# An attention forward and backward kernel on one core: its hand-written order of work replaced, from the first batch to the last

## The chip, the core and the metric

The kernel runs on one core of a Trainium2 chip. A core has a matrix engine (TensorE, PE in the profile, with its weight loads shown as PEld), a vector engine (VectorE, DVE), a scalar engine (ScalarE, ACT), a general engine (GpSimd, POOL) and a queue-only engine (SyncE, SP). 16 DMA engines move data between the chip's memory (DRAM) and the core's working memory (SBUF). Matmul results land in PSUM, here 8 banks of 2 KB in each of 128 partitions. The metric is device time in microseconds (us) for one launch. Three runs of the kernel before took 680.65, 680.86 and 682.24 us; the median is 680.86 us.

## The reference

Grouped-query attention with 32 batches, 32 query heads on 4 key heads, 4 queries and 2048 keys, head size 128, all in bf16; then its gradients.

```python
def _fwd_reference(q, k, v):              # q [32,32,4,128], k and v [32,4,2048,128]
    ...
    scores = jnp.einsum("bhqd,bhkd->bhqk", q, k) * scale
    p = _softmax(scores, axis=-1)
    return jnp.einsum("bhqk,bhkd->bhqd", p, v)

def reference(q, k, v, grad_out):
    ...
    _out, _vjp = jax.vjp(_f, q, k, v)
    return (out, dq, dk, dv)
```

In one batch K, V, dK and dV are 2 MB each, while q, grad_out, out and dq are 32 KB each, so a batch moves about 8.52 MB.

## The kernel before, in words

One batch is one unit of work. Its 32 x 4 queries fill the 128 partitions, 32 for each key head, and its 2048 keys are cut into two halves, called a (tile index 0) and b (tile index 1), of 1024 each. The kernel cuts the work of a batch into named items, each a Python function that issues a handful of instructions:

- LK and LV load K and V, four DMAs of 512 KB each on SP's queue (lines 226, 232). K has 3 buffers and V has 2 (lines 121, 122). The load of batch b+3's K waits for the last reader of batch b's K, which is dQ; V of batch b+2 waits for O of batch b. LV of batch 0 also issues, behind V, the q and grad_out rows of batches 1 to 3 (line 234); those of batch 0 come earlier on ScalarE's queue. Later groups of four batches are loaded by GpSimd inside LK (GROUP, lines 222 and 223), and a fence there makes GpSimd wait for them (line 221).
- QDT transposes q and grad_out of a batch (lines 245, 247).
- KT0 to KT7 and VT0 to VT7 each transpose an eighth of K or V: eight 128x128 transposes on TensorE into one bank (line 255) and one copy out of it (line 257). An even index needs key heads 0 and 1, an odd one heads 2 and 3.
- S makes the scores of a half (line 272) and their maximum (line 285). EX is the exponential on ScalarE, with the sum of a row (line 296). NRM inverts the sum (lines 311, 313), and GpSimd scales grad_out and q by it (lines 305, 316).
- ET and dST transpose the exponentials and the score gradients (lines 322, 324). O and dQ are the small products gathered over all keys, 64 matmuls each (line 338); O is followed by the sum called delta (line 365). dP forms a half's score gradient, ds (line 433).
- dV0 to dV7 and dK0 to dK7 each make an eighth of dV or dK: four matmuls into two banks (line 391) and a cast to bf16 in an SBUF tile (line 395). Indices 0 to 3 read half a, 4 to 7 read half b. When the eighth one is done, GpSimd issues the 2 MB store (lines 421, 188); for the last batch two stores of 1 MB go out. The dV and dK tiles share 4 buffers (line 129), so the first cast of a dK waits for the store of the dK two batches earlier.

Every engine works its own queue in the order in which the items are issued. Three strings give that order. HEAD lists the first three iterations with batch numbers. STEADY is one iteration, run for iterations 3 to 28; a "-" stands for the batch before, "+" for the batch after, "+2" for two after. TAIL lists the last three iterations, -1 being batch 31. The engine that empties a bank is in the name: a bare KT or VT copies on VectorE and one with "a" on ScalarE; a bare dV or dK casts on ScalarE and one with "d" on VectorE (lines 445 to 448). The class Banks hands out PSUM banks in issue order, the one longest free first. So an order also settles which earlier cast or copy each matmul group waits for.

Of the kernel before, what the change touches and what calls it, by code (L numbers as in the profile page):

```python
# [14 lines left out]


HEAD = """
LK@0 LV@0 KT4@0 KT6@0 KT2@0 KT0@0 QDT@0 KT3@0 KT1@0 KT5a@0 KT7@0 LK@1 LV@1 Sa@0 Sb@0 VT2a@0 VT4@0 VT0a@0 EXb@0 VT6@0 EXa@0 VT5@0 ETb@0 VT3@0 ETa@0
NRM@0 VT7a@0 VT1a@0 QDT@1 KT4@1 KT6@1 KT2a@1 KT0@1 KT3@1 dV7@0 O@0 dV5@0 dPb@0 dV1@0 KT5@1 KT1@1 dV3@0 dV6@0 dPa@0 KT7@1 dV2@0 LK@2 LV@2
VT2@1 dV4@0 Sa@1 dV0@0 Sb@1 dK7@0 VT5@1 VT3@1 EXb@1 dSTa@0 VT4@1 EXa@1 VT0@1 QDT@2 dSTb@0 KT4@2 dK1@0 dK6@0 KT6@2 KT2@2 KT0@2 NRM@1 dK0@0 dQ@0  # L20
dK3@0 dK5@0 dK2@0 ETb@1 ETa@1 VT7@1 KT3@2 VT6@1 VT1@1 dV7@1 dK4@0 O@1 dV5@1 dPb@1 dV1@1 KT5@2 KT1@2 dV3@1 dV6@1 dPa@1 KT7@2 dV2@1 LK@3 LV@3
VT2@2 dV4@1 Sa@2 dV0@1 Sb@2 dK7@1 VT5@2 VT3@2 EXb@2 dSTa@1 VT4@2 EXa@2 VT0@2 QDT@3 dSTb@1 KT4@3 dK1@1 dK6@1 KT6@3 KT2@3 KT0@3 NRM@2 dK0@1 dQ@1
dK3@1 dK5@1 dK2@1 ETb@2 ETa@2 VT7@2 KT3@3 VT6@2 VT1@2 dV7@2 dK4@1 O@2 dV5@2 dPb@2 dV1@2 KT5@3 KT1@3 dV3@2 dV6@2 dPa@2 KT7@3 dV2@2 LK@4 LV@4
VT2@3 dV4@2 Sa@3 dV0@2 Sb@3 dK7@2 VT5@3 VT3@3 EXb@3
"""
HEAD_ITERATIONS = 3
WARM_MATMULS = 23

STEADY = """
dSTa- VT4 EXa VT0 QDT+ dSTb- KT4+ dK1- dK6- KT6+ KT2+ KT0+ NRM dK0- dQ- dK3- dK5- dK2- ETb ETa VT7 KT3+ VT6 VT1  # L30
dV7 dK4- O dV5 dPb dV1 KT5+ KT1+ dV3 dV6 dPa KT7+ dV2 LK+2 LV+2 VT2+ dV4 Sa+ dV0 Sb+ dK7 VT5+ VT3+ EXb+
"""

TAIL = """
VT7@-3 VT6@-3 EXa@-3 dK5@-4 dSTa@-4 VT4@-3 NRM@-3 dSTb@-4 dK3@-4 KT0@-2 dK6@-4 KT6@-2 VT1@-3 dK4@-4 KT4@-2 dK1@-4 ETb@-3 KT1@-2 dK0@-4 ETa@-3 dQ@-4 QDT@-2 KT5@-2 dV5@-3
VT0@-3 dV1@-3 KT3@-2 O@-3 KT7@-2 dPa@-3 dV6@-3 dV7@-3 VT0@-2 KT2@-2 dV2@-3 dPb@-3 dK2@-4 VT4@-2 LK@-1 dSTa@-3 dV4@-3 dV0@-3 Sa@-2 dK1@-3 Sb@-2 dV3@-3 EXb@-2 VT3@-2
VT6@-2 VT5@-2 dSTb@-3 EXa@-2 dK3@-3 VT1@-2 ETb@-2 dK5@-3 NRM@-2 KT2@-1 dK7@-3 dQ@-3 LV@-1 VT2@-2 ETa@-2 dK0@-3 KT1@-1 dK4@-3 KT0@-1 KT6@-1 QDT@-1 dK2@-3 VT7@-2 O@-2
dV5@-2 dV3@-2 KT5@-1 dPa@-2 dV6@-2 KT4@-1 dK6@-3 KT3@-1 dV1@-2 dPb@-2 dV7@-2 KT7@-1 Sa@-1 dV2@-2 dV0@-2 Sb@-1 dV4@-2 dK1d@-2 dSTb@-2 EXb@-1 VT6@-1 EXa@-1 NRM@-1 dK7@-2  # L40
VT5@-1 dK4@-2 ETb@-1 VT1@-1 dK0@-2 VT7@-1 dK5@-2 dK3@-2 ETa@-1 dK6d@-2 dK2@-2 dV7@-1 VT0@-1 dV2d@-1 VT3@-1 dV5@-1 dSTa@-2 VT4@-1 O@-1 dV6@-1 dV4@-1 dV1d@-1 VT2@-1 dPb@-1
dV0@-1 dPa@-1 dV3@-1 dK4@-1 dQ@-2 dK3d@-1 dK2@-1 dK0d@-1 dK1@-1 dK5d@-1 dK7@-1 dK6@-1 dSTa@-1 dSTb@-1 dQ@-1
"""
TAIL_ITERATIONS = 3

# [457 lines left out]
```

## Time and profile before

| what | number |
|---|---|
| median of three runs | 680.86 us |
| the profiled execution | 680.64 us |
| its span, first to last instruction | 678.9 us |
| PE busy | 623.5 us, 92% |
| DVE busy | 589.8 us, 87% |
| ACT busy | 569.2 us, 84% |
| POOL busy | 273.0 us, 40% |
| moved by DMA | 274.45 MB, mean 404 GB/s |
| granted TensorE clock | 0.999 of full speed |

The profile is one execution of the kernel, and its page gives totals over the whole span. Stage by stage the numbers differ, so the trace is also read in windows, as a timeline of single instructions, and as a list of who waited for whom. In a timeline row the first number is the start and the second the time taken, x4 means four such instructions merged, and a bracket gives the idle time before them and what ended it ("issue" is idle time that nothing in the trace explains). Iteration 3 begins at about 69.5 us and the tail at about 605.3 us.

### The profile page before, as it was taken

The page shows a single profiled execution, that of the slowest core. Times are in us where ns is not written, and L with a number is a line of the kernel's source. Part 1 is how long each engine was busy: PE and PEld are TensorE (multiplying, and loading weights), DVE is VectorE, ACT ScalarE, POOL GpSimd, SP SyncE. Part 2 cuts the span into 40 slices and gives each one's busy share as a digit, 9 for nine tenths or more (in the row PEclk, how much of TensorE's full clock was granted, in tenths as well). Part 3 has the DMA queues.
Part 4 walks back from the last instruction along what each step waited for, and adds up shares of the span by engine and source line. Part 5 has one row for each costly group of instructions (what it writes and reads, how often), then busy time and mean ns, then how long its engine had stood idle before and what let it go on. Part 6 is the DMA issues. An engine that isn't in the chain of part 4 may idle for free.

```text
span 678.9 us, 28075 instructions
## 1 busy us (share of the span) xinstructions
PE 623.5 (92%) x12375; PEld 452.8 (67%) x12375; DVE 589.8 (87%) x997; ACT 569.2 (84%) x673; POOL 273.0 (40%) x457
## 2 busy tenths in 40 slices
PE   8999999999999989999999999999989899988984
PEld 6667776666776667776667776667666576655652
DVE  5889999988899888999989898988889888887895
ACT  3899889888888888989888888888888888886885
POOL 1353442544425444352545424364333643333310
PEclk9999999999999999999999999999999999999999
DMA  9999999999999999999999999999999999999888
GB/s 343 408 392 413 416 411 412 417 411 417 413 417 414 413 416 412 416 415 413 418 415 416 414 414 415 416 416 414 412 416 408 404 414 413 415 403 401 340 340 300
DMA packets 76970, 274.45 MB, mean 404 GB/s; under 512 B 8975, under 2 KB 9133, under 8 KB 76848
## 3 DMA queue, kind: packets, MB, share of 16 engines
q1 hardware_dynamic: 41920, 145.05, 53.3%
q0 software_dynamic: 34640, 127.55, 46.6%
q8 instruction: 96, 1.57, 0.8%
q14 instruction: 26, 0.21, 0.1%
q10 hardware_dynamic: 288, 0.07, 0.0%
HBM read 136.31 MB, written 136.31 MB: 402 GB/s over the span
## 4 chain that ended last, share of the span: by engine, by line
PE 70%; DMA 12%; ACT 6%; DVE 5%; issue 4%; POOL 1%; SPq 0%; ACTq 0%; DVEq 0%; POOLq 0%
PE banks L255 29%; PE banks L391 17%; PE banks L338 9%; DMA out_dram<-dk 8%; PE banks L322 8%; PE banks L272 7%; ACT dv L395 5%; DMA v_sb<-in_v_dram 2%; DVE ds L433 2%; DMA k_sb<-in_k_dram 1%; ACT dk L395 1%; DVE kt L257 1%; PE banks L245 1%; DVE dk L395 1%; DVE vt L257 1%
## 5 line engine op out<-in xcount | busy, mean ns | idle before, releaser
L395 ACT CAST dv<-banks 128x1024 bf16<-128x1024 f32 x254 | 244.2, 1026 | 56.6 <-PE banks L391 52.9
L395 ACT CAST dk<-banks 128x1024 bf16<-128x1024 f32 x251 | 246.1, 1022 | 22.1 <-PE banks L391 14.8
L257 DVE COPY kt<-banks 128x1024 bf16<-128x1024 bf16 x254 | 163.2, 680 | 12.1 <-PE banks L255 11.6
L257 DVE COPY vt<-banks 128x1024 bf16<-128x1024 bf16 x252 | 163.9, 681 | 1.4 <-PE banks L255 1.3
L305 POOL TENSOR_SCALAR dop<-do_sb,rinv 32x128 bf16<-32x128 bf16 x124 | 74.1, 598 | 200.4 <-PE banks L391 150.2
L255 PE MATMUL banks<-ident,v_sb 128*128 128x128 bf16 x2048 | 142.9, 219 | 12.7 <-ACT dv L395 10.2
L255 PE MATMUL banks<-ident,k_sb 128*128 128x128 bf16 x2048 | 143.6, 219 | 8.6 <-issue 5.9
L255 PEld LDWEIGHTS <-k_sb 128*128 128x128 bf16 x2048 | 119.3, 98 | 36.7 <-issue 34.8
L255 PEld LDWEIGHTS <-v_sb 128*128 128x128 bf16 x2048 | 121.3, 98 | 28.6 <-issue 25.9
L433 DVE SCALAR_TENSOR_TENSOR ds<-banks,delta,e 128x1024 bf16<-128x1024 f32 x64 | 82.0, 1283 | 25.9 <-PE banks L272 24.8
L391 PE MATMUL banks<-dop,e 64*128 64x256 bf16 x1024 | 96.2, 273 | 8.8 <-issue 3.2
L188 POOL DMA_DIRECT2D out_dram<-dv x56 | 39.2, 703 | 145.0 <-ACT dv L395 124.3
L391 PE MATMUL banks<-qp,ds 64*128 64x256 bf16 x1024 | 87.7, 271 | 2.4 <-DVE dk L395 1.2
L305 POOL TENSOR_SCALAR qp<-q_sb,srinv 32x128 bf16<-32x128 bf16 x128 | 77.7, 607 | 10.6
L296 ACT ACTIVATE e<-banks,negb 128x1024 bf16<-128x1024 f32 x64 | 70.8, 1112 | 9.8 <-DVE negb L288 9.7
L285 DVE TENSOR_REDUCE m<-banks 128x1 f32<-128x1024 f32 x64 | 75.1, 1215 | 0.7 <-PE banks L272 0.6
L391 PEld LDWEIGHTS <-e 64*128 64x128 bf16 x1024 | 34.1, 94 | 54.2 <-issue 37.5
L391 PEld LDWEIGHTS <-ds 64*128 64x128 bf16 x1024 | 41.9, 94 | 30.4 <-ACT dv L395 13.0
L324 DVE COPY et<-banks 128x1024 bf16<-128x1024 bf16 x64 | 41.8, 686 | 23.4 <-PE banks L322 22.9
L272 PE MATMUL banks<-vt,qdt 128*32 128x512 bf16 x512 | 41.3, 384 | 6.5 <-issue 4.8
L324 DVE COPY dst<-banks 128x1024 bf16<-128x1024 bf16 x64 | 43.4, 680 | 1.5 <-PE banks L322 1.5
L272 PEld LDWEIGHTS <-qdt 128*32 128x32 bf16 x1024 | 19.0, 94 | 35.2 <-issue 34.0
(45 smaller groups left out, 502.4 us busy)
## 6 DMA issues: line engine op xcount, KB each, us to landing
k_sb<-in_k_dram SPq DMA_DIRECT2D x128, 512.0 KB, 11.7
v_sb<-in_v_dram SPq DMA_DIRECT2D x128, 512.0 KB, 17.1
out_dram<-dk POOLq DMA_DIRECT2D x29, 2048.0 KB, 22.5
out_dram<-dv POOLq DMA_DIRECT2D x17, 2048.0 KB, 24.3
out_dram<-dv POOLq DMA_DIRECT2D x13, 1024.0 KB, 22.1
out_dram<-dv POOLq DMA_DIRECT2D x13, 960.0 KB, 25.5
out_dram<-dk SPq DMA_DIRECT2D x2, 2048.0 KB, 8.1
out_dram<-dv SPq DMA_DIRECT2D x1, 2048.0 KB, 9.0
```

The costliest lines, as they stand in the source:

```text
L255: nc.tensor.transpose(out=ps[:, 4 * hh + j, :], in_=S[which][:, 2 * (i % 2) + hh, 4 * (i // 2) + j, :], identity=ident[:])
L257: copy(out=S[f"{which}t{i}"][:], in_=ps)
L272: nc.tensor.matmul(ps[G * h:G * h + G, a, :], lhsT=S["qdt"][:, col, G * h:G * h + G], rhs=xt[:, 4 * (h % 2):4 * (h % 2) + 4, :].rearrange( ...
L285: nc.vector.reduce_max(out=S["m"][:, i:i + 1], in_=S[f"s{i}"][1], axis=AX.X)
L296: nc.scalar.activation(out=S[f"e{i}"][:], in_=ps, func=ACT.Exp, bias=S["negb"][:], scale=scale, accum_out=S["l"][:, i:i + 1],)
L305: engine.tensor_scalar(out=t[r, h % 2, :], in0=src[r, :], scalar1=by[r, :], scalar2=None, op0=ALU.mult)
L322: nc.tensor.transpose(out=ps[:, u, :], in_=S[f"{src}{i}"][:, P * u:P * u + P], identity=ident[:])
L324: nc.vector.tensor_copy(out=S[f"{name}{i}"][:], in_=ps)
L338: nc.tensor.matmul(ps[G * h:G * h + G, :], lhsT=S[f"{xt}{c // 8}"][:, c % 8, G * h:G * h + G], rhs=S[kv][:, h, c, :], start=(c == 0), stop ...
L391: nc.tensor.matmul(ps[:, a, :, c, :], lhsT=S[f"{x}{i // 4}"][r, u:u + P], rhs=S[y][r, :, :], start=True, stop=True, tile_position=(2 * G * ...
L395: copy(out=S[name][:, :, 2 * i:2 * i + 2, :].rearrange("p h c d -> p h (c d)"), in_=banks.ap(t).rearrange("p a (j w) -> p (a j) w", j=2),)
L433: nc.vector.scalar_tensor_tensor(out=S[f"ds{i}"][:], in0=ps, scalar=S["delta"][:], in1=S[f"e{i}"][:], op0=ALU.subtract, op1=ALU.mult,)
```

## The change

Only the three strings change; the functions and the amount of computation stay. In HEAD, STEADY and TAIL the same items stand in another order, and some change the engine that empties their banks.

```diff
 HEAD = """
-LK@0 LV@0 KT4@0 KT6@0 KT2@0 KT0@0 QDT@0 KT3@0 KT1@0 KT5a@0 KT7@0 LK@1 LV@1 Sa@0 Sb@0 VT2a@0 VT4@0 VT0a@0 EXb@0 VT6@0 EXa@0 VT5@0 ETb@0 VT3@0 ETa@0
-NRM@0 VT7a@0 VT1a@0 QDT@1 KT4@1 KT6@1 KT2a@1 KT0@1 KT3@1 dV7@0 O@0 dV5@0 dPb@0 dV1@0 KT5@1 KT1@1 dV3@0 dV6@0 dPa@0 KT7@1 dV2@0 LK@2 LV@2
-VT2@1 dV4@0 Sa@1 dV0@0 Sb@1 dK7@0 VT5@1 VT3@1 EXb@1 dSTa@0 VT4@1 EXa@1 VT0@1 QDT@2 dSTb@0 KT4@2 dK1@0 dK6@0 KT6@2 KT2@2 KT0@2 NRM@1 dK0@0 dQ@0
...
+LK@0 KT2@0 LV@0 KT6@0 QDT@0 KT0@0 KT4a@0 KT7@0 KT5a@0 LK@1 KT1@0 LK@2 KT3@0 QDT@1 Sb@0 VT2a@0 Sa@0 VT0a@0 VT6@0 VT1@0 EXa@0 VT7@0 EXb@0 VT3a@0 VT4@0
+LV@1 VT5a@0 ETa@0 NRM@0 KT2a@1 ETb@0 KT4@1 KT0a@1 KT6@1 O@0 KT5a@1 dPa@0 dV4@0 dPb@0 KT3a@1 dV3@0 LV@2 dSTa@0 KT7@1 dV6@0 dV0d@0 dK2@0 dV7@0 KT1@1 dV1d@0
+dV5@0 dSTb@0 Sa@1 dV2@0 Sb@1 dQ@0 VT3a@1 QDT@2 VT2@1 KT0@2 EXa@1 EXb@1 KT3@2 KT1@2 LK@3 NRM@1 VT6a@1 dK5@0 KT5@2 ETa@1 VT5@1 KT7a@2 ETb@1 VT1@1 VT4a@1
...
 STEADY = """
-dSTa- VT4 EXa VT0 QDT+ dSTb- KT4+ dK1- dK6- KT6+ KT2+ KT0+ NRM dK0- dQ- dK3- dK5- dK2- ETb ETa VT7 KT3+ VT6 VT1
-dV7 dK4- O dV5 dPb dV1 KT5+ KT1+ dV3 dV6 dPa KT7+ dV2 LK+2 LV+2 VT2+ dV4 Sa+ dV0 Sb+ dK7 VT5+ VT3+ EXb+
+dSTa- dSTb- VT7 VT0 EXa KT4a+ dQ- dK4- NRM dK6d- dK1- ETb VT6a KT0+ QDT+ dK3- dK5d- KT6+ dK2- VT1 dK0- ETa dV4 KT5+ dV6d dV1 VT4 LK+2
+dV3 O dV5 dPb dV7 dV0 LV+2 KT7+ KT3+ dV2 dPa KT1a+ KT2+ dK7 Sb+ VT2a+ Sa+ VT3a+ VT5+ EXb+
 """
...
 TAIL = """
...
-dV0@-1 dPa@-1 dV3@-1 dK4@-1 dQ@-2 dK3d@-1 dK2@-1 dK0d@-1 dK1@-1 dK5d@-1 dK7@-1 dK6@-1 dSTa@-1 dSTb@-1 dQ@-1
...
+dV6@-1 dV5@-1 dK0d@-2 VT0@-1 dV7@-1 VT7@-1 dK5@-2 dK6@-2 ETb@-1 dK1d@-2 VT1a@-1 VT2@-1 O@-1 dV1@-1 dV2@-1 dPa@-1 VT5@-1 VT4@-1 dV3@-1 dV0@-1 dK2@-1 dSTb@-2 dSTa@-2 dPb@-1 dK3@-1
+dK0@-1 dK1d@-1 dK4@-1 dK5@-1 dK6@-1 dK7d@-1 dQ@-2 dSTa@-1 dSTb@-1 dQ@-1
 """
```

Counted over the strings, an iteration of STEADY has 48 items before and after. ScalarE gets 5 copies of K and V (before 0) and VectorE 3 casts of dK and dV (before 0). HEAD has 153 items both times, with 21 such copies on ScalarE (before 6) and 9 such casts on VectorE (before 0). TAIL has 135 items, with 10 (before 0) and 12 (before 7). In HEAD batch 2's K is loaded ahead of batch 1's V, and QDT of batch 1 stands ahead of the scores of batch 0.

More of the change, by code (lines that the diff above doesn't have):

```diff
@@ L17 @@
 HEAD = """
-LK@0 LV@0 KT4@0 KT6@0 KT2@0 KT0@0 QDT@0 KT3@0 KT1@0 KT5a@0 KT7@0 LK@1 LV@1 Sa@0 Sb@0 VT2a@0 VT4@0 VT0a@0 EXb@0 VT6@0 EXa@0 VT5@0 ETb@0 VT3@0 ETa@0
-NRM@0 VT7a@0 VT1a@0 QDT@1 KT4@1 KT6@1 KT2a@1 KT0@1 KT3@1 dV7@0 O@0 dV5@0 dPb@0 dV1@0 KT5@1 KT1@1 dV3@0 dV6@0 dPa@0 KT7@1 dV2@0 LK@2 LV@2
-VT2@1 dV4@0 Sa@1 dV0@0 Sb@1 dK7@0 VT5@1 VT3@1 EXb@1 dSTa@0 VT4@1 EXa@1 VT0@1 QDT@2 dSTb@0 KT4@2 dK1@0 dK6@0 KT6@2 KT2@2 KT0@2 NRM@1 dK0@0 dQ@0
[L21 to L24, printed above, removed]
+LK@0 KT2@0 LV@0 KT6@0 QDT@0 KT0@0 KT4a@0 KT7@0 KT5a@0 LK@1 KT1@0 LK@2 KT3@0 QDT@1 Sb@0 VT2a@0 Sa@0 VT0a@0 VT6@0 VT1@0 EXa@0 VT7@0 EXb@0 VT3a@0 VT4@0
+LV@1 VT5a@0 ETa@0 NRM@0 KT2a@1 ETb@0 KT4@1 KT0a@1 KT6@1 O@0 KT5a@1 dPa@0 dV4@0 dPb@0 KT3a@1 dV3@0 LV@2 dSTa@0 KT7@1 dV6@0 dV0d@0 dK2@0 dV7@0 KT1@1 dV1d@0
+dV5@0 dSTb@0 Sa@1 dV2@0 Sb@1 dQ@0 VT3a@1 QDT@2 VT2@1 KT0@2 EXa@1 EXb@1 KT3@2 KT1@2 LK@3 NRM@1 VT6a@1 dK5@0 KT5@2 ETa@1 VT5@1 KT7a@2 ETb@1 VT1@1 VT4a@1
+VT0@1 dK3d@0 dV2@1 VT7@1 dV6@1 O@1 dV3@1 dPb@1 dV4@1 dV1@1 KT2@2 KT6@2 dV5@1 KT4@2 dV7@1 dPa@1 VT0a@2 Sb@2 dV0@1 Sa@2 dK0@0 KT7a@3 dSTa@1 dSTb@1 VT6@2
+EXa@2 VT5@2 EXb@2 NRM@2 VT1@2 dK6@0 dK1@0 dQ@1 dK4d@1 dK7@0 KT5@3 ETb@2 QDT@3 VT7a@2 dK2d@1 dK4@0 ETa@2 dK0@1 VT4@2 LV@3 dK3@1 KT3@3 KT6@3 dV7@2 dK7d@1
+dV3@2 O@2 dV4@2 dV0d@2 dV5@2 KT1@3 VT2a@2 dPb@2 dK1@1 VT3@2 LK@4 dK6d@1 KT0a@3 KT4@3 dV2@2 KT2a@3 dK5d@1 dV1@2 dPa@2 dV6@2 Sb@3 Sa@3 dK7@2 VT2a@3 VT3@3
+LV@4 VT5@3 EXb@3
 """
@@ L29 @@
 STEADY = """
-dSTa- VT4 EXa VT0 QDT+ dSTb- KT4+ dK1- dK6- KT6+ KT2+ KT0+ NRM dK0- dQ- dK3- dK5- dK2- ETb ETa VT7 KT3+ VT6 VT1
-dV7 dK4- O dV5 dPb dV1 KT5+ KT1+ dV3 dV6 dPa KT7+ dV2 LK+2 LV+2 VT2+ dV4 Sa+ dV0 Sb+ dK7 VT5+ VT3+ EXb+
+dSTa- dSTb- VT7 VT0 EXa KT4a+ dQ- dK4- NRM dK6d- dK1- ETb VT6a KT0+ QDT+ dK3- dK5d- KT6+ dK2- VT1 dK0- ETa dV4 KT5+ dV6d dV1 VT4 LK+2
+dV3 O dV5 dPb dV7 dV0 LV+2 KT7+ KT3+ dV2 dPa KT1a+ KT2+ dK7 Sb+ VT2a+ Sa+ VT3a+ VT5+ EXb+
 """
 TAIL = """
[L37 to L41, printed above, removed]
-dV0@-1 dPa@-1 dV3@-1 dK4@-1 dQ@-2 dK3d@-1 dK2@-1 dK0d@-1 dK1@-1 dK5d@-1 dK7@-1 dK6@-1 dSTa@-1 dSTb@-1 dQ@-1
+KT6@-2 dSTb@-4 dSTa@-4 VT7@-3 VT1@-3 EXa@-3 VT4a@-3 KT0@-2 NRM@-3 dK5@-4 dK6@-4 dQ@-4 VT0@-3 KT3@-2 dK0@-4 KT1@-2 dK2@-4 ETb@-3 QDT@-2 KT4@-2 dK4@-4 LK@-1 dV0@-3 ETa@-3 VT6@-3
+KT2@-2 dV6d@-3 dV5@-3 dV7@-3 O@-3 KT5a@-2 dPb@-3 dV1@-3 dPa@-3 dV4@-3 KT7@-2 QDT@-1 dV2@-3 LV@-1 dK3d@-4 dK1@-4 VT6a@-2 VT4@-2 Sb@-2 dV3@-3 dK2@-3 Sa@-2 KT0a@-1 KT4@-1 dSTa@-3
+KT6@-1 VT1@-2 EXb@-2 EXa@-2 VT3@-2 VT2@-2 dK5@-3 NRM@-2 ETb@-2 KT5a@-1 dK3@-3 KT1@-1 ETa@-2 KT2a@-1 VT5@-2 dK0d@-3 dK6@-3 VT7@-2 VT0a@-2 O@-2 dK7@-3 dV7d@-2 KT3a@-1 dPa@-2 dV5@-2
+dV3@-2 dSTb@-3 KT7@-1 dV1@-2 dK4d@-3 dV2@-2 dPb@-2 dK1@-3 dV4@-2 Sb@-1 dV0@-2 Sa@-1 dV6@-2 dK2d@-2 EXb@-1 EXa@-1 dK3d@-2 dQ@-3 dK7@-2 NRM@-1 VT6a@-1 dK4d@-2 ETa@-1 dV4@-1 VT3@-1
+dV6@-1 dV5@-1 dK0d@-2 VT0@-1 dV7@-1 VT7@-1 dK5@-2 dK6@-2 ETb@-1 dK1d@-2 VT1a@-1 VT2@-1 O@-1 dV1@-1 dV2@-1 dPa@-1 VT5@-1 VT4@-1 dV3@-1 dV0@-1 dK2@-1 dSTb@-2 dSTa@-2 dPb@-1 dK3@-1
+dK0@-1 dK1d@-1 dK4@-1 dK5@-1 dK6@-1 dK7d@-1 dQ@-2 dSTa@-1 dSTb@-1 dQ@-1
 """
```

## The prediction

> **What bounds the kernel now.** I first cut the span into stages (columns: start:end, length, then busy us and instruction count of PE, PEld, DVE, ACT, POOL, granted clock, DMA share, GB/s).
>
> ```profile
> 69.47:457.24 387.77, 365.68 (x7334) 267.22 (x7334) 346.65 (x590) 337.14 (x400) 171.25 (x280) 1.00 1.03 415
> 457.24:605.30 148.06, 134.53 (x2702) 98.40 (x2702) 127.20 (x218) 124.60 (x148) 60.89 (x100) 1.00 1.02 411
> 605.30:640.00 34.70, 32.20 (x660) 23.18 (x659) 29.40 (x51) 27.03 (x33) 13.74 (x24) 1.00 1.00 400
> 640.00:675.00 35.00, 27.32 (x524) 17.33 (x516) 29.23 (x44) 27.51 (x32) 3.14 (x6) 1.00 0.84 325
> ```
>
> In the steady stage the DMA engines are full: 415 GB/s, so a batch of 8.52 MB needs 20.5 us. The 26 iterations take (605.3-69.5)/26 = 20.6 us. TensorE is hardly slacker: 365.7 of 387.8 us. Only in the last 35 us do transfers wait for work, at 325 GB/s.
>
> Next the engines' own pace. By the timeline, iteration 274.41 to 294.25 took 19.84 us with one unexplained TensorE pause of 0.28 us ("issue"); such a pause comes once or twice an iteration, 0.3 to 1.0 us. Without it the order runs at 19.56 us. ScalarE waited for a store only four times:
>
> ```profile
> 490.22 1.01 ACT L395 CAST dv<-banks 128x1024 bf16<-128x1024 f32 x1 [1.93 <-DMA out_dram<-dv]
> 500.63 1.01 ACT L395 CAST dk<-banks 128x1024 bf16<-128x1024 f32 x1 [1.53 <-DMA out_dram<-dk]
> 541.99 1.01 ACT L395 CAST dk<-banks 128x1024 bf16<-128x1024 f32 x1 [0.22 <-DMA out_dram<-dk]
> 574.45 1.01 ACT L395 CAST dv<-banks 128x1024 bf16<-128x1024 f32 x1 [1.71 <-DMA out_dram<-dv]
> ```
>
> So engines and transfers run neck and neck. An order is worth what it changes in the head, in the pace, and in the tail.
>
> **The head: QDT of batch 1 ahead of the first scores.** The timeline of the first 20 us, and the page's DMA issues (last number: median us from issue to landing):
>
> ```profile
> 6.29 0.38 SPq L202 DMA_DIRECT2D q_sb<-in_q_dram  x1
> 6.72 0.49 SPq L202 DMA_DIRECT2D do_sb<-in_grad_out_dram  x1
> 8.72 1.74 PE L255 MATMUL banks<-ident,k_sb 128*128 128x128 bf16 x28 [0.51 <-DMA k_sb<-in_k_dram]
> 10.39 1.33 PE L272 MATMUL banks<-kt,qdt 128*32 128x512 bf16 x16
> 14.13 1.13 ACT L296 ACTIVATE e<-banks,negb 128x1024 bf16<-128x1024 f32 x1
> 17.85 0.22 PE L245 MATMUL banks<-ident,q_sb 128*128 128x128 bf16 x1
> ```
>
> ```profile
> q_sb<-in_q_dram SPq DMA_DIRECT2D x1, 96.0 KB, 9.0
> do_sb<-in_grad_out_dram SPq DMA_DIRECT2D x1, 96.0 KB, 8.9
> ```
>
> The rows of batches 1 to 3 are issued behind K and V of batch 0 and land at 6.29+9.0 = 15.3 and 6.72+8.9 = 15.6 us. Before, their first use is at 17.85, and the scores of batch 0 start at 10.39. In the new HEAD QDT@1 stands right after the eight KT@0 and before Sb@0. TensorE takes items in order, so from about 10.4 to 15.6 it stands still, with both S@0, all VT@0 and, through them, EX@0 behind it. By row durations: QDT 0.22, S 0.54, VT 0.45, S 0.54 put Sa at 17.1; about 0.7 from a score's first matmul to VectorE's start (309.62 to 310.36 in a dP); the maxima take 2.35, the negation 0.2; the first EX starts at about 19.3, not 14.13.
>
> From there I laid the items out by hand to Sb@1, each at the latest of its engine, inputs and bank. O@0 falls at 23.9 (before 21.5), dQ@0 at 34.0 (35.8), Sb@1 at 33.5 (28.4). VectorE's work up to Sb@1 is 22.3 us, before 21.9; ScalarE is 2.8 us ahead. What is left of the head for VectorE is 39.1 us, before 38.4, which took 41.1. So iteration 3 starts at about 75, **+5.4 us**; bounds +2.4 (O@0's delay, if ScalarE's lead is turned into time) and +6.5. The transfers do not cover this: K0, V0, K1, K2, V1, V2 last until 33.7, the dV store and K3 come at 34.8 and 35.1, and DMA idles about 2 us there, and 1.5 at the next two stores. K2 ahead of V1 costs nothing: V1 lands near 31 and is first read at 35.
>
> **The clock in that hole.** The last matmul ends at 672.86; the granted clock was 0.71 over 677 to 678 and 0.50 after:
>
> ```profile
> 676.00:677.00 1.00, 0.00 (x0) 0.00 (x0) 0.00 (x0) 0.00 (x0) 0.00 (x0) 1.00 0.50 166
> 677.00:678.00 1.00, 0.00 (x0) 0.00 (x0) 0.00 (x0) 0.00 (x0) 0.00 (x0) 0.71 0.03 8
> 678.00:678.90 0.90, 0.00 (x0) 0.00 (x0) 0.00 (x0) 0.00 (x0) 0.00 (x0) 0.50 0.00 0
> ```
>
> So it halved 4.6 us after the last matmul. The new hole is about 5.2 us: close. The two S and the VT between them, 1.5 us, would double on the way to EX: 0 to +1.5; I take **+0.6**. [...]
>
> **The steady order.** Sums of one iteration by row intervals: a transpose item 0.445 us, four dV or dK matmuls 0.22, S or dP 0.54, O or dQ 1.01, plus 0.10 to 0.13 at each change of matmul kind. Casts in a run on ScalarE come 0.935 us apart (five in 4.68), copies 0.92 (two in 1.93), casts on VectorE 1.14 (three in 3.49), copies there 0.61.
>
> ```profile
> 309.51 4.68 ACT L395 CAST dv<-banks 128x1024 bf16<-128x1024 f32 x5 [0.61 <-PE banks L391]
> 12.31 1.93 ACT L257 COPY vt<-banks 128x1024 bf16<-128x1024 bf16 x2 [1.25 <-PE banks L255]
> 667.42 3.49 DVE L395 CAST dk<-banks 128x1024 bf16<-128x1024 f32 x3 [1.51 <-PE banks L391]
> ```
>
> ScalarE, now 16 x 0.935 + 2 x 1.10 for EX + 0.4 for dQ's copy = 17.6: 17.6 + 5 x 0.92 - 3 x 0.935 = 19.4 us. VectorE, now 20 copies, 2 dP of 1.25, 2 maxima of 1.2 and 1.5 of small ones = 18.6: 18.6 + 3 x 1.14 - 5 x 0.61 = 18.9. TensorE: the dV and dK stand in 11 runs before and after, so grouping saves no changes; more transposes are followed by another kind (10 against 6), so 18.7 becomes 19.2. All fit into 20.5, but ScalarE's slack shrinks from 2.9 to 1.1 us. Laid out by hand over a whole iteration, the new order closes on itself at 19.63 us (ScalarE nearly gapless; EXb, which before waited 0.33 for the negation, now has two copies ahead of it). Against 19.56 that is 0.07, taken as 0.05, x 26 = **+1.3 us**. The ends are far apart: -0.4 an iteration (-10 us), if slack against the pauses lets engines reach the transfers' pace; +0.5 (+13), if ScalarE loses as much to waits as TensorE does now. I stay near the middle, the row it rests on being the old order's own 19.56.
>
> **Loads and stores.** LK waits for dQ, which moves from 5.9 to 3.4 us of TensorE work in the iteration; LV for O, which stays near 12. K then has about 18.6 us until its first transpose (before 15.8; median landing 11.7). GpSimd now issues dQ's store before NRM and the dK store after it, at about 10.5 us of an iteration, before 13.9; the dV store at 16.7, before 20. Counted to the first cast into the same buffer two batches later, a dK store may take 27.4 us (before 26.0), a dV store 33.9 (31.4). The four waits, 5.4 us, would nearly go. But full DMA engines are late next: time won there is partly waited elsewhere. I take half, **-2.7**; bounds 0 and -5.4.
>
> **The tail.** The same items; sums of TensorE, ScalarE, VectorE: before 55.9, 51.9, 55.5 us, after 53.6, 56.5, 55.1. Up to the last dV of batch 30 (before at 43 us of the tail) the largest sum falls from 37.8 to 36.1. From there to the last cast ScalarE grows from 18.5 to 20.4, past VectorE's 19.0: +1.4. After the last dP the old order still needs 7.4 us to its final dQ (665.9 to 673.3), the new one about 5.1, with the dV stores earlier. Together -2.6; I keep **-1.6**, as stores at 415 GB/s limit how far the end can follow. Bounds -6 (nearly all of the 7.6 us of transfer time lost at 325 GB/s) and +3.
>
> **Sum.** 5.4 + 0.6 + 1.3 - 2.7 - 1.6 = +3.0 on the profiled execution's 680.64: **683.6 us**, 2.7 above the median of 680.86.
>
> **The rivals.** *The transfers swallow the head's delay* (not slower): ScalarE, always with work queued, absorbs half of TensorE's pauses, the engines run at 20.1 us, and stores alone hold them back. They would reach the tail at 75 + 523 = 598, held by the transfers to about 601 instead of 605.3; with the tail's -1.6 about **676**. Where before 0.8 us an iteration was lost above 19.56, it needs a loss below 0.6. For it: both queues gain time, and 35 us of the tail are under-fed. Against: DMA loses some 3 us in the head.
> *ScalarE becomes the bound*: before, iterations up to 457.24 took 387.77/19 = 20.41 against a largest sum of 18.7, a loss of 1.7. On 19.4 that is 21.1, 0.5 above 20.6, x 26 = +13; with +5.4 for the head, no store waits (-5.4) and -1.6: **692**. It decides once ScalarE loses over 1.1 us an iteration. For it: 5 copies of 0.92 put on the engine with 16 casts. Against: the hand layout.
> *The head costs half*, and the rest cancels: **681**. For it: ScalarE's lead of 2.8 us at Sb@1.
>
> **Chances.** Forecast 0.42 (its own range 680.5 to 688), the swallowed delay 0.29, ScalarE bound 0.19, half the head 0.10. About 0.3%, 2.0 us, is what a measurement of this kernel can tell from no change. Faster by more: 0.30, nearly all from the second case; within it: 0.20; slower: 0.50. The range 674.5 to 692 takes in the centres of all cases and leaves out the far ends of the pace.
>
> **What would show it.** In the new profile: TensorE idle for some 5 us from 10.4 until do_sb lands; the first EX near 19 us; iteration 3 near 75; TensorE clock below 1 around 15 to 19. In the steady stage: ACT busy near 19.4 us an iteration; no or few ACT waits on out_dram; iterations of 20.5 to 20.7. Tail near 66 us instead of 67.6. I am wrong if the head's delay is made up before the tail starts (tail at 602 or earlier), or if ACT waits for PE more than 1.1 us in an iteration and iterations pass 21.

## The result and the profile after

The changed kernel takes 686.40 us (median of six runs, 684.28 to 687.24) against 681.19 us (six runs, 680.11 to 682.24): ratio 1.0065, 95% interval 1.0048 to 1.0082, so 4.4 us slower by the ratio (the medians lie 5.2 us apart). Its profiled execution took 684.28 us, with a span of 682.5 us against 678.9.

The head, from the timeline of the kernel after (start, length, engine, line, operation, count, and in brackets the idle time before it and what ended it):

```profile
14.08 0.29 PE L245 MATMUL banks<-ident,q_sb 128*128 128x128 bf16 x1 [3.50 <-DMA q_sb<-in_q_dram]
15.91 0.29 PE L245 MATMUL banks<-ident,do_sb 128*128 128x128 bf16 x1 [1.54 <-DMA do_sb<-in_grad_out_dram]
16.12 1.04 PE L272 MATMUL banks<-kt,qdt 128*32 128x512 bf16 x8
18.06 1.04 PE L272 MATMUL banks<-kt,qdt 128*32 128x512 bf16 x8
21.02 1.12 ACT L296 ACTIVATE e<-banks,negb 128x1024 bf16<-128x1024 f32 x1
```

TensorE stands still from 10.58 to 14.08 and again to 15.91, as the order said it would. But then eight matmuls of a score take 1.04 us where the prediction counted 0.54, and the first EX comes at 21.02. The windows of the same kernel tell why (the last three columns are granted clock, DMA share, GB/s):

```profile
12.00:13.00 1.00, 0.00 (x0) 0.00 (x0) 0.00 (x0) 0.00 (x0) 0.00 (x0) 1.00 0.98 340
13.00:14.00 1.00, 0.00 (x0) 0.00 (x0) 0.00 (x0) 0.00 (x0) 0.00 (x0) 0.91 1.28 316
14.00:15.00 1.00, 0.29 (x1) 0.10 (x1) 0.00 (x0) 0.00 (x0) 0.00 (x0) 0.50 0.96 381
19.00:20.00 1.00, 1.00 (x14) 0.96 (x11) 0.77 (x1) 0.18 (x1) 0.00 (x0) 0.50 1.02 406
20.00:21.00 1.00, 1.00 (x15) 1.00 (x14) 0.78 (x3) 0.89 (x1) 0.00 (x0) 0.68 1.09 434
...
30.00:35.00 5.00, 4.38 (x65) 3.02 (x62) 4.87 (x7) 4.92 (x6) 0.53 (x1) 1.00 0.88 353
35.00:40.00 5.00, 4.86 (x130) 4.06 (x126) 4.96 (x9) 4.10 (x6) 3.01 (x4) 1.00 0.45 108
40.00:45.00 5.00, 5.00 (x88) 4.45 (x84) 4.80 (x10) 4.73 (x7) 3.52 (x7) 1.00 1.00 369
```

The kernel before in one of these windows:

```profile
35.00:40.00 5.00, 5.00 (x135) 4.32 (x131) 3.94 (x9) 4.82 (x6) 2.25 (x4) 1.00 1.03 403
```

The clock halves from 13.8 to 20.6 us, long after TensorE has work again. Some 15 us later the transfers pay: between 35 and 40 us they move 108 GB/s (before 403), because the first loads are done and the first stores, delayed with the engines, are not yet there (the dV store of batch 0 is issued at 36.59 us, before at 30.12).

The steady stage, by windows of the kernel after:

```profile
200.00:350.00 150.00, 142.95 (x2789) 101.31 (x2786) 137.86 (x213) 139.94 (x169) 69.30 (x115) 1.00 1.03 415
350.00:500.00 150.00, 140.76 (x2786) 99.83 (x2783) 134.51 (x208) 137.47 (x164) 63.33 (x105) 0.99 1.03 415
```

Again 415 GB/s: this stage goes at the transfers' pace, and ScalarE (the fifth figure behind the stretch, counting its length) has grown from 17.8 to 19.1 us of a 20.6 or 20.7 us iteration. The K load that each iteration issues marks the pace. Where nothing held the engines, they ran at 19.5 us (101.14, 120.64, 140.13, 159.71, 179.27 us), faster than the old order ever did over four iterations; then iterations of 24.2 (404.15 to 428.31) and 23.4 us come between. The waits of the kernel after show what held them (total us, times, longest):

```profile
ACT dk L395 <- DMA out_dram<-dk: 13.1, 8, 3.2
ACT dv L395 <- DMA out_dram<-dv: 6.5, 4, 2.1
DVE dv L395 <- DMA out_dram<-dv: 2.8, 3, 1.3
```

The waits for stores, 5.4 us before, are now 22.4: engines that outrun the transfers are held where the next cast wants a buffer whose store has not landed. One such place, on the timeline of the kernel after:

```profile
421.73 1.01 ACT L395 CAST dk<-banks 128x1024 bf16<-128x1024 f32 x1 [3.15 <-DMA out_dram<-dk]
422.79 0.61 PE L255 MATMUL banks<-ident,v_sb 128*128 128x128 bf16 x8 [2.38 <-ACT dk L395]
```

TensorE stands 2.38 us behind the cast, and its clock is at 0.50 from 423.4 to 426.8 us.

The change in span, by K loads (those of iterations 3 and 28): up to the first, 79.74 against 76.53; between them 517.46 against 514.73, so 20.70 instead of 20.59 us an iteration, +2.7; from the second to the end 85.3 against 87.6. The load now stands some 2.5 us earlier in the iteration (3.4 instead of 5.9 us in), so the head is about +5.7 and the end about -4.8: +5.7 + 2.7 - 4.8 = +3.6.

A second ledger goes by transfers. Of all stretches, (1 - GB/s / 415.5) times the length is transfer time lost, added up here over stretches of 10 us; 415.5 GB/s is the rate of the full ones. The kernel before loses 4.2 us up to 90 us of the span, 2.0 between 90 and 590, 12.1 behind that; the kernel after 10.0, 2.0 and 9.9. The sum of such a ledger is the span less the 660.5 us that 274.45 MB take at that rate, so it says where time is lost and names no cause. With 2.0 us lost in the steady stage both times, nearly nothing can be made up there: what the head loses stays lost, unless the end gives it back.

### The profile page after: what moved, and what is told of

The parts are those of the page before. It is cut to its first block, busy times and chain, and to the rows that moved or that the text cites. A ratio compares the mean times of both kernels' runs of the same rounds, so it can differ in the third digit from the quotient of the medians.

```text
span 682.5 us, 28385 instructions
## 1 busy us (share of the span) xinstructions
PE 636.3 (93%) x12375; PEld 452.4 (66%) x12375; DVE 606.6 (89%) x934; ACT 616.0 (90%) x736; POOL 270.7 (40%) x454
## 3 DMA queue, kind: packets, MB, share of 16 engines
q8 instruction: 96, 1.57, 0.8%
## 4 chain that ended last, share of the span: by engine, by line
PE 44%; DMA 25%; DVE 13%; ACT 9%; issue 5%; POOL 1%; ACTq 0%; DVEq 0%; SPq 0%; POOLq 0%
PE banks L255 17%; DMA out_dram<-dv 15%; PE banks L391 12%; DMA out_dram<-dk 8%; PE banks L338 7%; DVE m L285 5%; PE banks L322 4%; DVE ds L433 3%; DVE kt L257 3%; PE banks L272 3%; ACT e L296 3%; ACT dv L395 3%; DMA do_sb<-in_grad_out_dram 2%; ACT vt L257 2%; ACT dk L395 1%
## 5 line engine op out<-in xcount | busy, mean ns | idle before, releaser
L395 ACT CAST dv<-banks 128x1024 bf16<-128x1024 f32 x225 | 216.1, 1050 | 17.8 <-PE banks L391 9.1
L395 ACT CAST dk<-banks 128x1024 bf16<-128x1024 f32 x188 | 185.5, 1061 | 19.3 <-DMA out_dram<-dk 13.1
L255 PE MATMUL banks<-ident,v_sb 128*128 128x128 bf16 x2048 | 150.9, 221 | 13.2 <-ACT dk L395 9.0
L257 DVE COPY kt<-banks 128x1024 bf16<-128x1024 bf16 x189 | 126.2, 682 | 11.0 <-PE banks L255 9.0
L257 DVE COPY vt<-banks 128x1024 bf16<-128x1024 bf16 x162 | 107.4, 681 | 8.0 <-PE banks L255 6.6
L257 ACT COPY vt<-banks 128x1024 bf16<-128x1024 bf16 x94 | 95.9, 1040 | 9.3 <-PE banks L255 8.8
L391 PE MATMUL banks<-dop,e 64*128 64x256 bf16 x1024 | 91.9, 274 | 8.1 <-ACT dv L395 6.0
L395 DVE CAST dk<-banks 128x1024 bf16<-128x1024 f32 x68 | 82.7, 1218 | 12.1 <-PE banks L391 12.1
L188 POOL DMA_DIRECT2D out_dram<-dq_sb x29 | 16.8, 578 | 158.0 <-ACT dq_sb L374 157.9
L257 ACT COPY kt<-banks 128x1024 bf16<-128x1024 bf16 x67 | 69.2, 1036 | 8.3 <-PE banks L255 7.9
```

The lines of the kernel that those rows point to most:

```text
L188: return (nc.sync if late() else nc.gpsimd).dma_start(**kw)
L255: nc.tensor.transpose(out=ps[:, 4 * hh + j, :], in_=S[which][:, 2 * (i % 2) + hh, 4 * (i // 2) + j, :], identity=ident[:])
L257: copy(out=S[f"{which}t{i}"][:], in_=ps)
L391: nc.tensor.matmul(ps[:, a, :, c, :], lhsT=S[f"{x}{i // 4}"][r, u:u + P], rhs=S[y][r, :, :], start=True, stop=True, tile_position=(2 * G * ...
L395: copy(out=S[name][:, :, 2 * i:2 * i + 2, :].rearrange("p h c d -> p h (c d)"), in_=banks.ap(t).rearrange("p a (j w) -> p (a j) w", j=2),)
```

## The experiments

The kernel before was run beside each group, and ratios are to it; 0.1% is 0.68 us. ± gives the half width of a 95% interval. Where a ratio is compared with that of the kernel after (another chip), both intervals are joined.

**QDT@1 moved back in the kernel after**

```
- ... KT3@0 QDT@1 Sb@0 ...  NRM@0 KT2a@1 ...
+ ... KT3@0 Sb@0 ...        NRM@0 QDT@1 KT2a@1 ...
```

> The kernel after with one item moved: QDT@1 stands behind NRM@0 instead of ahead of Sb@0, so TensorE does not stand still for the rows of batch 1. Theory H (the hole in the head costs the time: the delayed dV and dK stores leave the DMA engines short of work around 30 to 40 us, and a steady stage that runs at the transfers' pace cannot make it up): first EX near 14 us instead of 21.0, iteration 3 near 70 instead of 76, no slice near 108 GB/s at 35 to 40 us, time 680 to 681.5, 5 to 6.5 below the kernel after. Rival S (the steady order costs it, by 22.4 us of waits for stores in buffers, and would cost it whatever the head does): the engines only wait longer for stores, first EX near 14 all the same, but the time stays at 684.5 or more.

Measured: 681.02 us, ratio 0.9972 (0.9949 to 0.9994), 6.3 ± 1.9 us below the kernel after. The first EX is at 14.45 us, and the lost transfer time up to 90 us falls from 10.0 to 4.6. The waits for stores grew to 32 us, and yet the time fell: H holds for the head, S does not. The profiled execution took 684.29 us: what it gains in the head it loses again later (4.2 us of transfer time between 90 and 590, 13.2 behind that). So the shorter time is read from the twelve runs, and only the head from the trace.

**The hole alone, put into the kernel before**

```
- LK@1 LV@1 Sa@0 Sb@0 ... VT1a@0 QDT@1 KT4@1
+ LK@1 LV@1 QDT@1 Sa@0 Sb@0 ... VT1a@0 KT4@1
```

> The kernel before with the hole alone: QDT@1 moved right ahead of Sa@0, everything else as before. Theory H: first EX near 20 us, iteration 3 at 75 to 76, time 686 to 688, 5 to 6.5 above the kernel before, as the old order's steady stage has no faster pace to catch up with. Rival S: the hole by itself costs at most 2.5 us (up to 683.7), since ScalarE's and VectorE's slack in the head takes up the rest.

Measured: 689.38 us, ratio 1.0114 (1.0092 to 1.0136), +7.8 us. First EX at 20.82 us. Lost transfer time up to 90 us rises from 4.2 to 10.9. S falls; the price is above the 5 to 6.5 us of H. One item of two transposes, moved by fifteen places, costs more than the whole change.

**The hole filled, the wait kept**

```
+ if b == 1:                       # in QDT
+     t = banks.take(1)
+     for _ in range(40):
+         nc.tensor.matmul(banks.ap(t)[:, 0, 0:2 * D], ident, pairs["dop", 0] ...)
+     banks.give(t)
```

> The kernel after with 40 matmuls of 256 columns on data that nobody reads put ahead of QDT@1 (some 4.3 us at full clock), which fill TensorE's hole and keep its clock up, while the wait for the rows stays. It parts the clock from the wait. Theory H with a clock share of 1.7 us (first EX came at 21.0 instead of the 19.3 worked out without the clock): granted clock 1.00 from 12 to 21 us, first EX at 19.0 to 19.5, time 1 to 2 us below the kernel after (684.5 to 685.5). Rival W (the wait alone sets the head; what the clock costs is waited elsewhere): first EX earlier all the same, time within 0.7 us of the kernel after.

Measured: 682.82 us, ratio 1.0008 (0.9991 to 1.0024), 3.9 ± 1.6 below the kernel after, and 2.4 ± 1.9 above the one without the wait. The timeline of this kernel (its lines are 8 further on):

```profile
10.72 4.53 PE L247 MATMUL banks<-dop,ident 128*128 128x256 bf16 x40
15.08 0.22 PE L253 MATMUL banks<-ident,q_sb 128*128 128x128 bf16 x1
15.29 0.61 PE L280 MATMUL banks<-kt,qdt 128*32 128x512 bf16 x8
18.67 1.11 ACT L304 ACTIVATE e<-banks,negb 128x1024 bf16<-128x1024 f32 x1
```

The scores take 0.61 us again, the clock stays at 1.00, and the first EX comes 2.35 us earlier. Of that, 0.83 us is not the clock: in this execution the rows landed at about 15.0 us, as the forty matmuls ended, and the scores began at 15.29 instead of 16.12. From the first score to the first EX it is 3.38 us here and 4.90 in the kernel after, so on this path the half clock costs 1.5 us, the upper bound of the prediction. Forty useless matmuls make the kernel faster, by more than the 1 to 2 us of H. W falls.

How the hole's price divides is not settled. By the times the clock has the larger part, 3.9 against 2.4 us, with intervals that overlap. By the traces it has the smaller or an equal one: the lost transfer time up to 90 us is 10.0 in the kernel after, 7.9 here and 4.6 without the wait, and the dV store of batch 0 is issued at 36.59, 33.99 and 31.29 us. And the hole in the kernel before had half as long a stretch of half clock, 3.4 us (15.58 to 18.99), and cost 7.8 us.

**All rows of the first group loaded at once**

```
-         rows(g, 0, W if g else 1, queue)
+         rows(g, 0, W, queue)
...
-        if b == 0:
-            rows(0, 1, W, nc.sync)
```

> The kernel after with the q and grad_out rows of all four batches of the first group loaded at once, ahead of V of batch 0, instead of batch 0's ahead and those of batches 1 to 3 behind K and V of batch 0; the order of the items is untouched. Theory H: the rows land by about 8 us, QDT@1 finds its input, first EX at 14 to 14.5, time 680 to 682 as with QDT@1 moved. Rival R (the 192 KB more of short rows hold back K and V of batch 0, which all transposes wait for): first EX at 15.5 or later, and the time 683 or more.

Measured: 679.91 us, ratio 0.9982 (0.9962 to 1.0001), 5.7 ± 1.8 below the kernel after, with its order of items untouched. First EX at 14.79 us, a little behind H's 14 to 14.5. R falls. So the order was not bad in itself: it used rows that the loads brought too late.

**Heads, steady orders and tails of the two kernels mixed**: each kernel takes its HEAD, STEADY and TAIL strings from one or the other.

Old head, new steady order, new tail:

> Head of the kernel before, steady order and tail of the kernel after. Theory H (head hole costs, steady at the transfers' pace, tail pays back): 681.2 less the tail's gain of 3 to 4.5, so 676.5 to 678.5. Rival S (the new steady order costs through store waits): 681 or more, iterations of 20.7 or more.

Measured: 680.63 us, ratio 0.9985 (0.9966 to 1.0003), 5.4 ± 1.7 us below the kernel after: the head's price again. But H had 2 to 4 us less, and 681 was where S began; the new steady order must cost something too.

New head, old steady order, old tail:

> Head of the kernel after, steady order and tail of the kernel before. Theory H: the head's full price with nothing paid back, 686.5 to 689 (iteration 3 near 76). Rival S: 683 to 684, since the old steady order is the better one.

Measured: 687.32 us, ratio 1.0077 (1.0052 to 1.0102): the head costs 5.2 ± 1.7 us. As H had it.

Only the steady order new:

> Head and tail of the kernel before, only the steady order of the kernel after. Theory H (both orders run at the transfers' pace): 680 to 682, within 1 us of the kernel before, tail starting at 604 to 606. Rival S: 683 to 686, tail starting at 607 or later. Rival F (the faster engine pace of 19.5 us does bring time): 678 or less, tail starting at 602 or earlier.

Measured: 686.21 us, ratio 1.0059 (1.0040 to 1.0078), +4.0 ± 1.3. H said no change, and S has its number. But the place is not the one that S named: the lost transfer time is 2.7 us between 90 and 590 us (before 2.0), and 19.7 behind that (before 12.1). In the profiled execution TensorE stands from 602.0 to 604.5 us as the tail begins, within the 64 matmuls of one O; no wait for a store is near (the last one before it ends at 577.98 us), and the clock halves at 605.8:

```profile
604.47 0.24 PE L338 MATMUL banks<-v_sb,et 128*32 128x128 bf16 x4 [2.45 <-issue]
```

The last K load then comes at 623.62 us, before at 615.85. What such a pause goes with, the last section shows. This execution took 689.62 us, 3.4 above the median of its twelve runs, so how much of the +4.0 us comes from such a pause, and whether the old tail follows badly on the new steady order, stays open.

Only the tail new:

> Head and steady order of the kernel before, only the tail of the kernel after. Theory H: 676.5 to 678.5, tail near 63 to 64 us instead of 67.6. Rival T (the short tail of the kernel after, 63 us, came from stores that lay further behind or ahead when it began, not from its order): 680 to 681.5.

Measured: 678.32 us, ratio 0.9947 (0.9930 to 0.9963): -3.6 ± 1.1 us, **the fastest kernel of all, ahead of both**. T falls. The windows of the kernel before and of this one, in this order:

```profile
640.00:645.00 5.00, 4.95 (x76) 2.58 (x69) 4.05 (x8) 4.55 (x5) 0.51 (x1) 1.00 0.54 219
650.00:655.00 5.00, 4.40 (x60) 2.93 (x57) 4.79 (x13) 5.00 (x8) 2.54 (x5) 1.00 1.02 410
655.00:660.00 5.00, 4.46 (x76) 3.25 (x79) 4.90 (x8) 4.09 (x5) 0.09 (x1) 1.00 0.48 191
```

```profile
640.00:645.00 5.00, 4.43 (x61) 2.06 (x58) 4.99 (x7) 5.00 (x7) 0.00 (x0) 1.00 0.53 219
650.00:655.00 5.00, 4.79 (x66) 3.21 (x64) 4.95 (x8) 5.00 (x7) 2.16 (x4) 1.00 1.03 412
655.00:660.00 5.00, 5.00 (x128) 3.59 (x126) 4.48 (x8) 4.35 (x5) 0.00 (x0) 1.00 0.99 376
```

Both run dry at 640 us; only the old tail does it again at 655, where the new one already has a half of batch 31's dV to store (issued at 654.70 us, in the old tail at 663.20). At 190 instead of 376 GB/s for 5 us, that is 2.2 us.

Head and tail new, steady order old:

> Head and tail of the kernel after, only the steady order of the kernel before: it tells what the new steady order is worth inside the change. Theory J (the new order gains nothing while the transfers bind, and comes to the tail with stalls behind it, as with the old head, where it cost 2.6 us with the new tail and 4 with the old): 682.5 to 684.5, 2 to 4 below the kernel after. Rival H (with the late head there is slack for the faster engines to use): 686 to 688, the kernel after or above.

Measured: 684.27 us, ratio 1.0033 (1.0014 to 1.0052), 2.2 ± 1.7 below the kernel after. J holds. With the old head and the new tail, the new steady order costs 2.6 ± 1.7 us (ratios 0.9985 against 0.9947).

**The transfers taken off the limit**

```
-                store(out=dst[b][r, h, :], in_=o[r, h])
+                store(out=dst[b][r, h, :] if name == "dv" else dst[b][r, 0:1, :],
+                      in_=o[r, h] if name == "dv" else o[r, 0:1])
```

> The kernel before, which writes of dK only key head 0 in batches 0 to 30: three quarters of those dK are left out of the output. A batch then moves some 6.95 MB instead of 8.52, 16.7 us at 415 GB/s, so that the engines and not the transfers set the steady pace. If the engines of the old order by themselves need 20.0 to 20.2 us an iteration (the stretches without store waits in its trace), 665 to 672. If they need the 19.56 laid out by hand, 655 to 660.

Measured: 696.35 us, ratio 1.0235 (1.0174 to 1.0296). The four runs are 690.63, 691.43, 701.28 and 701.72 us; the kernel before beside it has a median of 682.22 and no run above 684.73. That it is slower is plain, how much is not: the lower two are only 1.3% above. No figure that was written down comes near: with 18% less to move, the old order is slower than with all of it. No wait for a store is left; iterations take 21.2 us (K loads from 76.5 to 605.4). TensorE's pauses that no other engine ends ("issue") add up to 31.7 us from 70 to 590 us, before 14.9:

```profile
PE banks L255 <- issue: 17.1, 15, 2.6
```

What these pauses go with, the last section shows; why they are longer with less to move, these runs don't show.

> The kernel after with the same three quarters of dK left out of the output. Theory E (the new steady order is the faster one for the engines, 19.5 against 20.0 to 20.2 us, and only the transfers keep that from showing): 10 to 17 us below the kernel before with the same left out, iterations of 19.5 to 19.6 throughout, no waits on stores. Rival N (both orders have the same engine pace, as the hand layouts of 19.56 and 19.63 said): 1 to 5 us above it.

Measured: 670.83 us, ratio 0.9802 (0.9754 to 0.9849); the four runs are 664.09, 669.45, 672.22 and 675.67 us. The mean of the lower three is 22 us below that of the lower two of the kernel before with the same left out, so E has the sign, and more than its 10 to 17 us, because the old order was slower than any bound given. In the profiled execution, that of 675.67 us, iterations take 19.5 to 19.8 us from 99 to 256 us, and later 19.5 to 23.2, not 19.5 to 19.6 throughout as E had it. N falls: with these bytes left out, the new order is much the faster.

**dK7 later in the steady order (old head, new tail)**

```
-KT1a+ KT2+ dK7 Sb+ VT2a+ Sa+ VT3a+ VT5+ EXb+
+KT1a+ KT2+ Sb+ VT2a+ Sa+ VT3a+ VT5+ dK7 EXb+
```

> Head of the kernel before, steady order and tail of the kernel after, with one item of the steady order moved: dK7, the first cast into the dK buffer of a batch, goes from ahead of Sb of the next batch to just ahead of EXb, some 2.5 us later, so that the store of two batches before has that much longer. It is to be read beside the kernel with the old head and the dK7 left in place (680.6). Theory L (the waits for dK stores, with the half clock behind the long ones, are what the new order costs): waits of ScalarE and VectorE for dK stores fall from 20.8 us to below 10, time 677.5 to 679. Rival B (the transfers bind, so a wait taken away here comes back at the next one): the waits on stores of dK and dV together stay above 15 us, or the time is lost elsewhere, time 680 to 681.5.

Measured: 685.74 us, ratio 1.0057 (1.0031 to 1.0083), 4.9 ± 2.2 us above the kernel with dK7 left in place. The waits for stores are gone altogether, none instead of 26.9 us, and it is slower. Its iterations take 20.5 us from the start, since TensorE now waits 0.5 us for a copy in each of 26 iterations:

```profile
PE banks L391 <- ACT vt L257: 12.9, 26, 0.5
```

L falls: less waiting for stores did not mean less time, so these waits are a sign of engines that run ahead. B, by which they would come back, did not describe it either: the place of one cast moved the engines' own pace by a whole microsecond, from 19.5 us, below the transfers' pace, to level with it. That this leaves no lead for a late store or a pause, and that this is where the 4.9 us went, is argued and not shown; and since the edit slowed the engines as well, what the store waits by themselves cost has not been isolated.

## Why the prediction was nearly right, and where it was not

It said 683.6 us; the result, 686.4, lies within its range. In like terms it said +3.0 us on the profiled execution, which became +3.6 (684.28 against 680.64). That the sum is this close is partly luck: against the experiments, the steady stage was put 3.6 to 5.4 us too low and the tail 1.4 to 3.4 us too high.

- **Head, +5.4 and clock +0.6, together +6.0.** Measured 5.2 ± 1.7 (new head alone), 5.4 ± 1.7 (old head put back), 6.3 ± 1.9 (QDT@1 moved). The place, the rows waited for and the low transfers in the thirties were as said, and so is the sum of the two terms. The split was not. The wait, worked out as +5.4, costs 2.4 ± 1.9 by the times and 3.3 us of lost transfer time; the clock costs 3.9 ± 1.6 and 2.1. So the term that was mis-sized most is the clock's, +0.6. The one fall at the kernel's end, 4.6 us after the last matmul, left it open whether the clock would fall at all, so less than half of the 1.5 us was taken, and nothing for what is slow behind the first EX. Here it fell 3.2 us after the last matmul and stayed low for 6.8 us: 1.5 us up to the first EX, and more behind it. The first EX was worked out at 19.3 without the clock; with the scores' start at 16.12 and 3.38 us from there at full clock it would have come at 19.5, and it came at 21.02.
- **Pace, +1.3, and loads and stores, -2.7.** Together -1.4; measured +2.2 ± 1.7 and +2.6 ± 1.7 with the new tail, +4.0 ± 1.3 with the old head and tail, +2.7 in the trace. This is the step with the wrong sign. "The four waits, 5.4 us, would nearly go" took the age of a buffer in the order's own time. But a faster order (19.5 us where nothing holds it) against 20.5 us of transfers catches up with its stores, and then waits: 22.4 us. That time is not simply the price: the kernel with QDT@1 moved back waited 32 us and took less. What the new steady order does cost beyond the transfers' pace appears, in the traces with the old head, behind 590 us: 10.4 us of lost transfer time against 8.8 with the new tail, 19.7 against 12.1 with the old, the 19.7 in an execution that has a pause of its own there. How the stalls and half clocks of the steady stage turn into a late end is not settled.
- **The hand layout, 19.63 against 19.56 us.** The 19.63 was right: 19.5 in free stretches. The 19.56 was not what the old order does: 20.6 us, with 14.9 us of TensorE's "issue" pauses in the steady stage against 3.7 in the new. The layout took such a pause off as if it were chance; as the last section shows, the order settles where such pauses fall. An order laid out without gaps says what it could do, not what it does.
- **Tail, -1.6.** Right in kind (dV stores earlier, a shorter end), too small: -3.6 ± 1.1 alone, -5.0 ± 1.8 and -3.0 ± 2.1 in the other mixes, about -4.8 in the trace of the kernel after. The first sum, -2.6, had been cut because stores at 415 GB/s limit how far the end can follow; the second dry stretch at 655 us, which goes, was not looked for.
- **The rivals.** The swallowed delay got its engines, even faster ones than the 20.1 us it needed, and still fell: its path back led through transfers that had no slack. The tail did not begin at 601 us: iteration 28's K load came 5.9 us later than before, at 597.20 instead of 591.26. ScalarE did not become the bound: 19.1 us of 20.7.

## What to carry to other kernels

Where a steady stage runs at the transfers' pace, judge an order by the transfer time that its head and its tail leave unused; here a faster order in between bought waits for stores. Before an item is moved ahead in an in-order engine, look up when its operands land: here one early pair of transposes cost 5 to 8 us, and an earlier load of 192 KB gave it back. Price such a hole with the clock behind it, in full stretches of half speed: here one or two of 3.4 us. And before an unexplained pause is taken for chance, count the instructions up to it.

## What the runs showed of the hardware

**Half-clock stretches of one length.** Eleven falls of the clock in eight of the kernels, between 330 and 610 us, were followed from half microsecond to half microsecond: every one lasted 3.40 to 3.42 us; in the head of the kernel after it was 6.83, two of them. Within one trace the falls and rises lie whole numbers of 3.413 us apart, in the kernel after at 13.81, 20.64, 423.41, 426.82, 583.84 and 587.25 us: 573.44 us from the first to the last, 168 times 3.4133. And the stall ahead could be short. With the rows loaded at once, TensorE was idle for 1.8 us:

```profile
408.91 2.84 ACT L393 CAST dv<-banks 128x1024 bf16<-128x1024 f32 x3 [1.98 <-DMA out_dram<-dv]
409.98 0.40 PE L389 MATMUL banks<-dop,e 64*128 64x256 bf16 x4 [1.81 <-ACT dv L393]
```

The clock halved at 410.55, when TensorE had been at work again for half a microsecond, and was full again at 413.96. So an idle time shorter than the stretch that followed was enough, 1.8 us here and 2.4 in the kernel after (ended at 422.79). Stalls of 1.57 and 1.62 us in the kernel after (ended at 338.40 and 507.76 us) were followed by no fall. Taken in steps of 3.413 us from each trace's own falls, from 25 us to the last matmul, the fourteen traces show how much idle time in one step went with a fall at its end: all 12 steps in which TensorE's busy time left 1.95 us or more idle were followed by a fall, 7 of 35 with 1.49 to 1.89, and none of 2607 with less. In the kernel after, the step ahead of the fall at 423.41 us left 2.38 us idle, that ahead of the fall at 583.84 us 1.99, and the one from 505.33 us, with 1.62, had none behind it.

**What TensorE's longer "issue" pauses are.** The profile's views name nothing that ends them, but the traces show where they fall and what landed ahead of them. Behind 25 us, the fourteen traces have 200 places where two matmuls start more than 0.45 us apart with no semaphore waited for between them. All 200 are at the same place of a count: between the 95th and the 96th of every 128 matmuls, which with their weight loads make 256 instructions. The page lists a DMA queue of the kind "instruction" (packets, MB, share of the DMA engines' time):

```profile
q8 instruction: 96, 1.57, 0.8%
```

That is one packet of 16 KB for each such place, and every one of the 200 pauses ended 1.15 to 1.61 us after a packet of this kind had landed. So TensorE was, by these signs, waiting for its next instructions; that is read from the count and the packets, and no row of a trace names the wait. In the kernel before, the next packet starts 3.6 us (median) after such a place and takes 0.95; with some 1.4 us more, 256 instructions that are done in less than about 6 us would end in a wait (an estimate from these three figures). An iteration has 386 matmuls, three times 128 and two, so from one iteration to the next the places hardly move, and the order settles which items they fall on: kernels with the old steady order have 19 to 26 such pauses, those with the new one 3 to 13.

**Fewer bytes, more time.** The old order with three quarters of dK not stored took more time than with all of it, 1.3% by its lower two runs and 2.3% by the ratio, as told above. So the engines' pace was no fixed number of the order.
